# A limit of four on the weight transfers in flight in a streamed attention-and-mixer kernel

## Chip, cores and metric

One core of one Trainium2 chip. The metric is the device time of one execution in microseconds (us), as the median of several runs.

## The reference, cut to what matters

Four layers over 2048 tokens of width 640: attention with a recurrent memory, a token mixer with an MLP, and both again with the same weights. The attention works in 64 segments of 32 tokens, each one with 8 memory rows that come out of the segment before:

```python
for s in range(n_seg):                       # 64 segments, one after the other
    h = concat([mem, x[segment s]])          # 8 + 32 = 40 rows
    q, k, v = h @ Wq, h @ Wk, h @ Wv         # 32 heads of 192: 6144 columns each
    o = softmax(mask(q k^T * scale)) v @ Wo
    mem = o[:8]; outs.append(o[8:])
```

The four attention matrices together are 31 MB, and each segment needs all of them. The kernel keeps part of them resident on the core and streams the rest from HBM again in every step.

## The kernel before

The two attention layers run as two lanes, five segments apart, side by side in one step (80 columns); the first and last five steps have one lane (40 columns). All operations are first recorded with an engine, an estimated duration and a due time. A small list scheduler, the plan, then lays them out with a model of the transfers, and that order becomes each engine's program. Weights go through a ring of 8 slots. SyncE issues each transfer in the plan's order, as soon as the slot's former contents have been used.

```python
RING = 8
DMA_RATE = 345.0e3      # bytes per us in the plan
DMA_LAT = 2.2           # us
DMA_SKEW = 2.4          # us from the mean end of service to the last engine's landing
...
        def est(o, t):                       # earliest start of o in the plan
            s = max(t, o.ready)
            ...                              # and when its slots are free
...
            if o.dma:
                srv = max(s + DMA_LAT, srv) + o.dma / DMA_RATE
                done = srv + DMA_SKEW        # successors and slots count from here
...
            b = ring("ra")                   # streamed weights: 2 chunks of 128 x 768, 384 KB
            def fn(op):
                nc.sync.dma_start(out=T(b)[:, 0:2 * n].rearrange("p (c n) -> p c n", c=2), in_=w_src(kind, g, a, a + 2))
            add("SP", 0.45, due, fn, w=(b,), dma=P * 2 * n * 2, queue="wa")
...
    placed = plan.place()
    ctx.enter_context(tc.manual_schedule())
    for o in placed:
        o.fn(o)
```

## Time and profile before

| | before |
|---|---|
| median time | 3617.45 us (3604 to 3626) |
| span of the profiled run | 3600.4 us |
| middle stage, both lanes | 302 to 3299 us |
| transfers on SyncE's queue, all weights but two | 2941, one per 1.22 us |
| time from issue to landing | 5.3 us |

A transfer "lands" with the last of the sixteen increments of its semaphore, in the trace of before 1.95 us (median) after the first. "In flight" counts the transfers that are issued and not landed. "Idle" of TensorE is counted between one matmul's start and the next beyond the median distance for that form. I put it down to an instruction fetch where the instruction is the first of a block of 256 and no semaphore came in just before, and to weights where the last semaphore to come in was that of a weight transfer. The lines themselves stand in the prediction.

A line of waits reads: engine, what it writes, source line, then what ended the wait, then us in total, times, longest. PE is TensorE, PEld its weight loads, DVE VectorE, ACT ScalarE, POOL GpSimd, SPq SyncE issuing transfers. `wst` is a slot of the weight ring; `psq`, `psk`, `psv` and `psy` take the products with Wq, Wk, Wv and Wo, and `psh` and `y` those of the mixer. "issue" stands for idle time that nothing in the profile ended.

### The profile page before, as it was taken

What the parts mean: (1) busy time and instruction counts of PE and PEld (TensorE: products, weight loads), DVE (VectorE), ACT (ScalarE), POOL (GpSimd) and SP (SyncE); (2) the same over time, 40 slices, a digit from 0 to 9 for tenths busy, and PEclk for the clock granted to TensorE, in tenths of its full rate; (3) what the DMA queues carried; (4) which work ended last, traced back from release to release, by engine and by line L of the source; (5) the groups of instructions that cost most, each with busy time, mean ns of one, the idle gap of its engine ahead of it and who ended that gap; (6) DMA issues with size and microseconds to landing.
All of it is one profiled execution on the core that took longest, in us unless ns stands there. A gap on an engine that the chain in (4) does not pass through costs nothing.

```text
span 3600.4 us, 187964 instructions
## 1 busy us (share of the span) xinstructions
PE 3389.2 (94%) x84703; PEld 3261.4 (91%) x84703; DVE 2379.7 (66%) x7085; ACT 1703.7 (47%) x3584; POOL 305.4 (8%) x522
## 2 busy tenths in 40 slices
PE   5889999999999999999999999999999999999896
PEld 4778999999999999999999999999999999998785
DVE  2456766766666767666766677676767776676555
ACT  2344544544445555444545455554545554454432
POOL 2000000000000000000000000000000000000000
PEclk9999999999999999999999999999999999999998
DMA  9999999999999999999999999999999999999996
GB/s 343 301 307 311 304 304 299 310 301 303 297 307 314 311 298 309 300 301 305 315 308 309 298 304 313 308 307 307 308 311 311 313 309 301 301 307 310 297 314 211
DMA packets 804790, 1097.16 MB, mean 305 GB/s; under 512 B 51982, under 2 KB 800540, under 8 KB 803984
## 3 DMA queue, kind: packets, MB, share of 16 engines
q1 hardware_dynamic: 795472, 1069.06, 90.8%
q0 software_dynamic: 8512, 16.08, 1.4%
q8 instruction: 662, 10.85, 1.2%
q14 instruction: 144, 1.18, 0.1%
HBM read 1079.68 MB, written 8.19 MB: 302 GB/s over the span
## 4 chain that ended last, share of the span: by engine, by line
PE 89%; issue 5%; DMA 3%; DVE 1%; ACT 1%; SPq 0%; POOL 0%; POOLq 0%; ACTq 0%; DVEq 0%
PE psy L669 16%; PE psk L530 16%; PE psv L571 16%; PE psq L530 16%; PE psvt L583 5%; PE pso L650 5%; PE pss L602 4%; PE psh L993 3%; PE y L1011 3%; PE pst L635 2%; DMA wst<-in_A_Wq_dram 1%; PE psh L939 1%; PE hs L961 1%; DMA wst<-in_A_Wv_dram 1%; PE psv L755 1%
## 5 line engine op out<-in xcount | busy, mean ns | idle before, releaser
L656 DVE CAST oT<-pso 128x480 bf16<-128x480 f32 (+1 forms) x552 | 342.0, 620 | 478.0 <-PE pso L650 472.3
L587 ACT COPY V<-psvt 80x768 bf16<-80x768 bf16 (+1 forms) x552 | 438.4, 794 | 350.4 <-PE psvt L583 348.8
L530 PEld LDWEIGHTS <-wst 128*128 128x128 bf16 x13248 | 549.8, 100 | 37.4 <-issue 25.3
L669 PE MATMUL psy<-oT,wo 128*128 128x80 bf16 (+1 forms) x10350 | 499.6, 199 | 22.0 <-issue 14.8
L571 PE MATMUL psv<-hT,wv 128*128 128x80 bf16 (+1 forms) x9936 | 467.6, 199 | 15.7 <-issue 14.1
L530 PE MATMUL psq<-hT,wq 128*128 128x80 bf16 (+1 forms) x9936 | 463.4, 199 | 19.7 <-issue 12.7
L538 ACT CAST qT<-psq 128x480 bf16<-128x480 f32 (+1 forms) x552 | 292.1, 529 | 379.0 <-PE psq L530 375.6
L530 PE MATMUL psk<-hT,wk 128*128 128x80 bf16 (+1 forms) x9936 | 452.1, 199 | 19.0 <-issue 16.1
L577 ACT CAST vTs<-psv 128x480 bf16<-128x480 f32 (+1 forms) x552 | 291.8, 529 | 346.9 <-PE psv L571 340.9
L669 PEld LDWEIGHTS <-wo 128*128 128x128 bf16 x10350 | 418.7, 99 | 28.4 <-issue 20.6
L530 PEld LDWEIGHTS <-wk 128*128 128x128 bf16 x9936 | 398.2, 99 | 35.5 <-issue 21.4
L530 PEld LDWEIGHTS <-wq 128*128 128x128 bf16 x9936 | 400.6, 99 | 30.9 <-issue 14.4
L571 PEld LDWEIGHTS <-wv 128*128 128x128 bf16 x9936 | 400.3, 99 | 30.3 <-issue 16.6
L613 DVE CUSTOM_DVE_ANT_1 pss<-pss,mask 80x320 f32<-80x320 f32 (+1 forms) x512 | 245.0, 479 | 210.8 <-PE pss L602 206.4
L571 PE MATMUL psv<-hT,wst 128*128 128x80 bf16 (+1 forms) x6624 | 354.3, 199 | 13.0 <-issue 10.5
L530 PE MATMUL psk<-hT,wst 128*128 128x80 bf16 (+1 forms) x6624 | 349.8, 199 | 16.9 <-issue 12.9
L669 PE MATMUL psy<-oT,wst 128*128 128x80 bf16 (+1 forms) x6210 | 342.5, 199 | 6.9 <-issue 6.4
L530 PE MATMUL psq<-hT,wst 128*128 128x80 bf16 (+1 forms) x6624 | 331.8, 199 | 11.7 <-issue 7.4
L640 ACT COPY PT<-pst 80x320 bf16<-80x320 bf16 (+1 forms) x552 | 221.8, 402 | 249.3 <-PE pst L635 248.2
L625 DVE TENSOR_REDUCE sm<-pss 80x4 f32<-80x320 f32 (+1 forms) x552 | 252.1, 457 | 126.4 <-ACT pss L620 125.9
L546 DVE CAST kT<-psk 128x320 bf16<-128x320 f32 (+1 forms) x552 | 254.5, 461 | 105.4 <-PE psk L530 98.0
L620 ACT ACTIVATE pss<-pss,sm 80x320 f32<-80x320 f32 (+1 forms) x552 | 261.6, 474 | 123.1 <-DVE sm L613 123.0
(117 smaller groups left out, 5270.2 us busy)
## 6 DMA issues: line engine op xcount, KB each, us to landing
wst<-in_A_Wk_dram SPq DMA_DIRECT2D x552, 384.0 KB, 5.4
wst<-in_A_Wq_dram SPq DMA_DIRECT2D x552, 384.0 KB, 5.4
wst<-in_A_Wv_dram SPq DMA_DIRECT2D x552, 384.0 KB, 5.2
wst<-in_A_Wo_dram SPq DMA_DIRECT2D x621, 320.0 KB, 5.0
wst<-wbd SPq DMA_DIRECT2D x280, 320.0 KB, 5.2
wst<-in_B_w_dram SPq DMA_DIRECT2D x280, 320.0 KB, 5.8
wst<-wbd SPq DMA_DIRECT2D x70, 160.0 KB, 4.8
wk<-in_A_Wk_dram SPq DMA_DIRECT2D x8, 576.0 KB, 10.4
```

The lines of the kernel that those rows point to most:

```text
L530: nc.tensor.matmul(out=o[:, c, 0:N], lhsT=w[:, c * P:(c + 1) * P], rhs=h[:, kc, c0:c0 + N], start=pq.begin(), stop=True, skip_group_check= ...
L538: nc.scalar.copy(out=q[:, :, 0:N], in_=T(pq)[:, :, 0:N])
L546: nc.vector.tensor_copy(out=k4[:, :, 0::3, 0:N], in_=p4[:, :, 0::2, 0:N])
L571: nc.tensor.matmul(out=o[:, c, 0:N], lhsT=w[:, c * P:(c + 1) * P], rhs=h[:, kc, c0:c0 + N], start=pv.begin(), stop=True, skip_group_check= ...
L577: nc.scalar.copy(out=vs[:, :, 0:N], in_=T(pv)[:, :, 0:N])
L587: nc.scalar.copy(out=V_[0:N, :, 0:Dh], in_=T(pt)[0:N].rearrange("n c f -> n (c f)").rearrange("n (i e) -> n i e", i=HG))
L613: nc.vector.tensor_tensor_reduce(out=o, in0=o, in1=maskt.unsqueeze(1).to_broadcast([N, HG, N]), scale=-scale, scalar=3.0e38, op0=ALU.add, ...
L620: nc.scalar.activation(out=o, in_=o, func=ACT.Exp, bias=sm_[0:N, 0:1], scale=-1.0)
L625: nc.vector.reduce_sum(out=sm_[0:N, 4:4 + HG], in_=o, axis=AX.X)
L640: nc.scalar.copy(out=Pt[0:N, :, 0:N], in_=T(pst)[0:N, :, 0:N])
L656: nc.vector.tensor_copy(out=o_[:, :, 0:N], in_=T(pso)[:, :, 0:N])
L669: nc.tensor.matmul(out=T(psy[j])[:, m - m0, c0:c0 + N], lhsT=w[:, m * P:(m + 1) * P], rhs=o_[:, c, 0:N], start=psy[j].begin(), stop=True, ...
```

## The change

The intent, in the change's own words: "At most four weight transfers in flight: each waits for the landing of the fourth one ahead of it; placement plans with that". The plan also believes in an earlier landing (skew 1.0 instead of 2.4 us).

```diff
-DMA_SKEW = 2.4
+DMA_SKEW = 1.0
+FLIGHT = 4
...
         def est(o, t):
             s = max(t, o.ready)
+            if o.dma and o.e == "SP" and len(landed) >= FLIGHT:
+                s = max(s, landed[-FLIGHT])
...
                 done = srv + DMA_SKEW
+                if e == "SP":
+                    landed.append(done)
...  (each fn of a SyncE transfer now returns its instruction)
+    flight = []
     for o in placed:
-        o.fn(o)
+        ins = o.fn(o)
+        if o.dma and o.e == "SP":
+            if len(flight) >= FLIGHT:
+                tc.add_manual_dep(ins.ins, flight[-FLIGHT].ins.name,
+                                  mybir.DependencyInfo(mybir.DependencyClass.Sync, mybir.DependencyReason.DATA),
+                                  reason="transfers in flight")
+            flight.append(ins)
```

More of the change, by code (lines that the diff above doesn't have):

```diff
@@ L155, in place @@
         srv = 0.0
+        landed = []
         out = []
@@ L428, in fn @@
                 def fn(op):
-                    nc.sync.dma_start(out=tl[:], in_=w_src(kind, g, 0, cut))
+                    return nc.sync.dma_start(out=tl[:], in_=w_src(kind, g, 0, cut))
                 add("SP", 0.45, due, fn, w=(b,), dma=P * cut * n * 2, queue="wa")
@@ L438, in fn @@
             def fn(op):
-                nc.sync.dma_start(out=T(b)[:, 0:2 * n].rearrange("p (c n) -> p c n", c=2), in_=w_src(kind, g, a, a + 2))
+                return nc.sync.dma_start(out=T(b)[:, 0:2 * n].rearrange("p (c n) -> p c n", c=2), in_=w_src(kind, g, a, a + 2))
             add("SP", 0.45, due, fn, w=(b,), dma=P * 2 * n * 2, queue="wa")
@@ L462, in fn @@
             def fn(op):
-                nc.sync.dma_start(out=T(b)[:, 0:(e - a) * Dm].rearrange("p (c n) -> p c n", n=Dm), in_=src)
+                return nc.sync.dma_start(out=T(b)[:, 0:(e - a) * Dm].rearrange("p (c n) -> p c n", n=Dm), in_=src)
             add("SP", 0.45, due, fn, r=rd, w=(b,), dma=P * (e - a) * Dm * 2, queue="wb")
@@ L1052, in f1 @@
         def f1(op):
-            nc.sync.dma_start(out=xo[0:M, :], in_=A_mem0[0])
+            return nc.sync.dma_start(out=xo[0:M, :], in_=A_mem0[0])
         add("SP", 0.1, -90, f1, w=(B("xo"),), dma=20000)
@@ L1067, in f4 @@
         def f4(op):
-            nc.sync.dma_start(out=vb[:], in_=x0d[0:4 * SEG, :])
+            return nc.sync.dma_start(out=vb[:], in_=x0d[0:4 * SEG, :])
         add("SP", 0.1, -91, f4, w=(B("vb"),), dma=P * Dm * 2)
```

## The prediction

> **What bounds the kernel now.** I read the page first: the busy times, the 40 slices, the queues and the chain that ended last.
>
> ```profile
> PE 3389.2 (94%) x84703; PEld 3261.4 (91%) x84703; DVE 2379.7 (66%) x7085; ACT 1703.7 (47%) x3584; POOL 305.4 (8%) x522
> PE   5889999999999999999999999999999999999896
> DMA  9999999999999999999999999999999999999996
> GB/s 343 301 307 311 304 304 299 310 301 303 297 307 314 311 298 309 300 301 305 315 308 309 298 304 313 308 307 307 308 311 311 313 309 301 301 307 310 297 314 211
> q1 hardware_dynamic: 795472, 1069.06, 90.8%
> q8 instruction: 662, 10.85, 1.2%
> PE 89%; issue 5%; DMA 3%; DVE 1%; ACT 1%; SPq 0%; POOL 0%; POOLq 0%; ACTq 0%; DVEq 0%
> ```
>
> TensorE looks full, the DMA engines look full, and the chain is 89% TensorE, 5% "issue" and 3% DMA. The 5% is the surprise, so I looked for what TensorE waits for, in the long middle stage (302 to 3299 us from the start) where every step carries both lanes (80 columns):
>
> ```profile
> PEld L530 <- issue: 47.6, 61, 2.2
> PE psk L530 <- issue: 21.1, 32, 1.6
> PE psq L530 <- issue: 18.0, 22, 2.1
> PE psv L571 <- issue: 17.3, 27, 1.7
> PEld L530 <- DMA wst<-in_A_Wk_dram: 0.8, 2, 0.4
> ```
>
> Weights almost never arrive late (0.8 us in the largest such row); the idle time has no releaser at all. The timeline around 1011 us shows one of these gaps, in the middle of one run of matmuls from a resident weight tile:
>
> ```profile
> 1011.44 0.20 PE L571 MATMUL psv<-hT,wv 128*128 128x80 bf16 x1
> ...
> 1012.30 0.77 PE L571 MATMUL psv<-hT,wv 128*128 128x80 bf16 x17 [0.66 <-issue]
> 1012.31 0.63 PEld L571 LDWEIGHTS <-wv 128*128 128x128 bf16 x16 [0.76 <-issue]
> ```
>
> Nothing in the data can be late there, so I counted TensorE's instructions (weight loads and matmuls in order) and compared with the instruction queue, q8: 662 packets of 16 KB. TensorE has some 169,400 instructions; over 662 that is 256 each. Of the 150 gaps over 300 ns in the middle stage, 132, holding 112.8 of 119.4 us, sit exactly where one block of 256 ends and the next begins. They are instruction fetches that came late. Taking each form of matmul at its median start-to-start time, the middle stage holds 2861 us of matmuls in 2997 us; about 110 us of the missing 136 are fetch stalls, 2 us are waits for weights. In the two 40-column stages (104 to 302 and 3299 to 3498 us) fetch stalls are 20 and 19 us. So the whole kernel has about 150 us of them, 4% of its time.
>
> Next, the weight transfers themselves:
>
> ```profile
> SPq L439 <- PE psy L669: 346.7, 330, 3.6
> SPq L439 <- PE psv L571: 334.9, 331, 4.1
> SPq L439 <- DMA wst<-in_A_Wk_dram: 6.3, 14, 1.6
> ...
> wst<-in_A_Wk_dram SPq DMA_DIRECT2D x552, 384.0 KB, 5.4
> wst<-in_A_Wo_dram SPq DMA_DIRECT2D x621, 320.0 KB, 5.0
> ```
>
> SyncE, which issues them, waits for TensorE to give a ring slot back, hardly ever for another transfer. A transfer takes about 5.3 us to land. 2941 of them in 3600 us is one per 1.22 us, so on average 5.3 / 1.22 = 4.3 are in flight. Record by record (issue, and the last of the transfer's semaphore increments), an issue in the middle stage finds 4 or more ahead of it in 66% of cases (4: 37%, 5: 25%, 6: 3%). The landed weights then lie about 3.2 us (median) before TensorE's first wait on them.
>
> [...] 136 of 566 crossings of the middle stage stall by over 0.2 us, and a block of 256 runs in 5.1 us here. [...] the fetch of a block starts 1.3 to 3.3 us (10th to 90th percentile, median 2.3) after TensorE enters the block before it, never long before. [...] here a fetch starts later the more weights are in flight (below). [...]
>
> **The change, part by part.** (1) Each transfer on SyncE's queue waits for the landing of the fourth ahead. No data moves differently; the built program has the same number of instructions on each engine but for some 490 semaphore waits on SyncE, which is idle anyway (issues take 0.37 us of each 1.22). Two thirds of the issues are put off, by about the time until the oldest lands, some 0.5 us.
>
> What it removes is queue ahead of the fetch. For the 566 blocks of the middle stage, by weights in flight when TensorE enters the block before: with 3 in flight the fetch starts after 1.5 us and the mean stall is 52 ns (77 blocks); with 4, 2.0 us and 84 ns (196); with 5, 2.5 us and 293 ns (187); with 6, 2.7 us and 351 ns (87). A fetch takes 1.0 us and its block starts 1.2 us after it at the earliest, so in a block of 5.1 us a start later than 2.9 us stalls; the trace shows stalls from 2.6 us up. With at most 4, I take the mean of the 3 and 4 rows, 75 ns, against 193 now: 566 x 0.118 = 67 us. In the 40-column stages the same split is thinner; I take 15 of their 37 us. Together about 80 us off TensorE, which sets the end there.
>
> (2) The plan believes in an earlier landing: 1.4 us less (2.4 to 1.0). It therefore sets uses closer behind landings and counts on slots sooner. The order does change: 61% of TensorE's positions hold the same instruction. Of the 3.2 us of slack, 1.4 are planned away and about 0.5 are lost to the later issue, less what a shorter queue gives back. The early tail of slack (5% below 1.0 us, 10% below 1.4) turns into waits: I estimate 10% of 2941 transfers by 0.1 us, 30 us. (3) The real latency should fall to about 4.5 us, so the plan's new figure is nearer to the truth, and in the 40-column stages, where TensorE has 36 us of matmuls in a step of 49.5, a shorter slot cycle may give a few us: 10 us in all. Sum: 3617 - 80 + 30 - 10 = 3557; I round to 3550, as the author's smaller skew looks fitted.
>
> **The rivals.** *The limit itself becomes the bound.* With four in flight, one lands per latency / 4. Issues that now find 3 ahead just after a landing (137 of them) take 4.95 us: 1.24 us per transfer, against the 1.22 needed today and 1.19 for my time. All 2941 at 1.24 would be 3650 us plus the ends, about 3680. For it: DMA is at 9 tenths everywhere. Against it: with 4 or more ahead, landings follow each other at 1.12 us on average (median 1.08), so 4 x 1.12 = 4.5 us of queued work covers the lone latency of 3.3 us; and the windows show 369 to 372 GB/s between 20 and 80 us against 305 later, so the engines have reserve. *Nothing happens*: the fetch is held up by the DMA being full, not by the number in flight, and the rows with 5 and 6 merely mark busy moments. Then fetch stalls stay at 150 us and the time within 1% of 3617. The steady rise from row to row speaks for the queue, but it is a correlation. *The plan gains more*: if fetch stalls nearly vanish and 40-column steps shorten by 4 us each, 3617 - 140 - 40 = 3440.
>
> **Range and chances.** Fetch savings of 40 to 130 us and new weight waits of 0 to 80 span 3475 to 3650. The 2% line is at 3545, close to my point, so faster by over 2% and within 2% are near even, and the limit as the new bound keeps some chance of slower: 0.48, 0.40, 0.12.
>
> **What would show it.** Right: TensorE's "issue" idle time in the middle stage falls to about a third to a half; the median time to landing of 384 KB falls from 5.4 to 4.5 us; SyncE's waits name DMA landings in hundreds of rows; waits of TensorE for weights rise by tens of us, not hundreds. Wrong: "issue" stays while landings get quicker (then it was not the queue ahead), or TensorE's rows name "DMA wst" for over 100 us and GB/s falls below 300 (then the limit binds).

The figures are from the trace of before; in all 566 blocks of its middle stage the fetch began only after TensorE had entered the block ahead, by 0.24 us at the least. The lone latency of 3.3 us is a miscount: the trace shows 3.02 and 2.96 us.

## The result and the profile after

The changed kernel takes 3724.37 us (3715.65 to 3744.81, 4 runs) against 3618.78 us for the kernel before on the same chip: ratio 1.0305, 95% interval 1.0252 to 1.0358. Ratios here and below are the mean time of one kernel's fast runs over the mean of the other's in the same rounds, so not quite the ratio of the medians quoted. It is slower by 3%, outside my range of 3475 to 3650 us.

The page of the changed kernel, the same lines as those shown of before:

```profile
PE 3424.1 (92%) x84703; PEld 3279.1 (88%) x84703; DVE 2372.3 (64%) x7085; ACT 1717.9 (46%) x3584; POOL 306.0 (8%) x522
GB/s 323 305 300 302 299 295 294 297 296 301 307 301 290 295 290 292 292 293 297 294 296 297 294 299 296 304 295 296 297 301 292 289 297 297 296 305 300 304 298 202
PE 56%; DMA 40%; issue 2%; DVE 0%; POOL 0%; ACT 0%; SPq 0%; POOLq 0%; DVEq 0%
wst<-in_A_Wk_dram SPq DMA_DIRECT2D x552, 384.0 KB, 4.8
```

The chain that ended last now runs through DMA for 40% of the span, where it was 3%. Each transfer lands sooner (4.8 us, not 5.4), and yet the rate is lower in nearly every slice. "DMA" is a full row of nines in both pages, so that row would have shown nothing.

TensorE's waits in the changed kernel's middle stage (306 to 3401 us), then SyncE's waits over the whole run:

```profile
PE y L1017 <- DMA wst<-in_B_w_dram: 59.9, 35, 3.1
PE psh L999 <- DMA wst<-wbd: 30.3, 40, 2.0
PE psk L536 <- DMA wst<-in_A_Wk_dram: 26.8, 40, 1.7
PE psy L675 <- DMA wst<-in_A_Wo_dram: 23.0, 22, 2.6
...
PE psk L536 <- issue: 0.5, 1, 0.5
```

```profile
SPq L445 <- DMA wst<-in_A_Wq_dram: 342.5, 407, 3.3
SPq L445 <- DMA wst<-in_A_Wv_dram: 333.7, 406, 2.8
...
SPq L445 <- PE psy L675: 113.0, 167, 1.9
```

The "issue" rows of before are all but gone (0.5 us in the row for psk, where it was 21.1), and rows that name weights stand in their place (158 us together). SyncE, which waited for TensorE to give slots back, now waits for landings. (The line numbers are six higher in this kernel.)

Taken matmul by matmul, the middle stage shows both effects at full size:

| middle stage, us | before | after |
|---|---|---|
| length | 2997 | 3095 |
| matmuls at their median distance | 2861 | 2866 |
| late instruction fetches | 110.6 | 6.7 |
| late weights | 2.0 | 200.0 |
| ScalarE and VectorE | 16.1 | 2.7 |
| put down to none of these | 7 | 20 |

The matmuls at their median distance take 2860 to 2872 us in this stage in every run of this document, so TensorE's own pace explains none of the differences.

The middle stage thus loses 98 of the 114 us by which the profiled spans differ; the rest is in the ramp (4.8), the second 40-column stage (5.3) and the drain (5.5).

### The profile page after: what moved, and what is told of

It is laid out like the page before. It is cut to its first block, busy times and chain, and to the rows that moved or that the text cites. A ratio compares the mean times of both kernels' runs of the same rounds, so it can differ in the third digit from the quotient of the medians.

```text
span 3714.0 us, 188436 instructions
## 1 busy us (share of the span) xinstructions
PE 3424.1 (92%) x84703; PEld 3279.1 (88%) x84703; DVE 2372.3 (64%) x7085; ACT 1717.9 (46%) x3584; POOL 306.0 (8%) x522
## 3 DMA queue, kind: packets, MB, share of 16 engines
q14 instruction: 148, 1.21, 0.1%
## 4 chain that ended last, share of the span: by engine, by line
PE 56%; DMA 40%; issue 2%; DVE 0%; POOL 0%; ACT 0%; SPq 0%; POOLq 0%; DVEq 0%
PE psy L675 11%; DMA wst<-in_A_Wk_dram 11%; PE psv L577 10%; PE psq L536 9%; PE psk L536 9%; DMA wst<-in_A_Wq_dram 7%; DMA wst<-in_A_Wv_dram 7%; DMA wst<-in_B_w_dram 6%; DMA wst<-wbd 5%; DMA wst<-in_A_Wo_dram 5%; PE psvt L589 3%; PE pso L656 3%; PE pss L608 3%; PE y L1017 2%; PE psh L999 2%
## 5 line engine op out<-in xcount | busy, mean ns | idle before, releaser
L577 PE MATMUL psv<-hT,wv 128*128 128x80 bf16 (+1 forms) x9936 | 494.4, 199 | 4.6 <-issue 2.2
L675 PE MATMUL psy<-oT,wo 128*128 128x80 bf16 (+1 forms) x10350 | 491.6, 199 | 6.5 <-DMA wo<-in_A_Wo_dram 4.9
L536 PE MATMUL psk<-hT,wk 128*128 128x80 bf16 (+1 forms) x9936 | 473.3, 199 | 7.2 <-DMA wk<-in_A_Wk_dram 4.9
L577 PEld LDWEIGHTS <-wv 128*128 128x128 bf16 x9936 | 415.1, 99 | 19.5 <-DMA wv<-in_A_Wv_dram 3.3
L536 PEld LDWEIGHTS <-wk 128*128 128x128 bf16 x9936 | 407.3, 100 | 20.5 <-DMA wk<-in_A_Wk_dram 5.6
L577 PE MATMUL psv<-hT,wst 128*128 128x80 bf16 (+1 forms) x6624 | 343.4, 200 | 21.5 <-DMA wst<-in_A_Wv_dram 20.0
```

The lines of the kernel that those rows point to most:

```text
L536: nc.tensor.matmul(out=o[:, c, 0:N], lhsT=w[:, c * P:(c + 1) * P], rhs=h[:, kc, c0:c0 + N], start=pq.begin(), stop=True, skip_group_check= ...
L577: nc.tensor.matmul(out=o[:, c, 0:N], lhsT=w[:, c * P:(c + 1) * P], rhs=h[:, kc, c0:c0 + N], start=pv.begin(), stop=True, skip_group_check= ...
L675: nc.tensor.matmul(out=T(psy[j])[:, m - m0, c0:c0 + N], lhsT=w[:, m * P:(m + 1) * P], rhs=o_[:, c, 0:N], start=psy[j].begin(), stop=True, ...
```

## The experiments

Theory A: the wait itself caps the rate. With n in flight one transfer can land per (time to landing) / n, and with four this is more than TensorE needs. Theory B: the smaller skew makes the plan set uses too early, so that TensorE waits for weights whatever the limit. The first four runs take the two halves of the change apart and loosen the limit. In all of them the constant in the plan and that of the wait are separate:

```diff
-            if o.dma and o.e == "SP" and len(landed) >= FLIGHT:
-                s = max(s, landed[-FLIGHT])
+            if o.dma and o.e == "SP" and len(landed) >= PLAN_FLIGHT:
+                s = max(s, landed[-PLAN_FLIGHT])
```

"9999" below switches a limit off.

**Limit alone.** Every engine's instructions stand in the order of the kernel before (compared on all five engines); only the waits are added.

```diff
+PLAN_FLIGHT = 9999
+FLIGHT = 4
+DMA_SKEW = 2.4
```

> The old plan (skew 2.4, no limit in it), so every engine's order is that of the kernel before; only the wait for the landing of the fourth ahead is added. Theory A (the limit caps the rate: latency / 4): 3680 to 3740 us, median landing of 384 KB 4.8 us, TensorE's waits for weights in the middle stage 150 to 220 us, fetch stalls there under 15 us. Theory B (the new plan's smaller skew sets the uses too early): about 3550 us, fetch stalls gone as in the changed kernel, waits for weights under 30 us, because the old order keeps 3.2 us of slack.

Measured: 3692.61 us, ratio 1.0237 (1.0205 to 1.0270), as theory A had it in each number. In the middle stage TensorE waits 170.8 us for weights and 9.0 us for fetches. Landing takes 4.84 us on average, and 91% of the issues start within 0.15 us of the landing of the fourth ahead (median 0.063 us after it). The waits of TensorE in its middle stage:

```profile
PE psk L537 <- DMA wst<-in_A_Wk_dram: 57.4, 64, 2.2
PE psv L578 <- DMA wst<-in_A_Wv_dram: 34.6, 48, 1.5
PE y L1018 <- DMA wst<-in_B_w_dram: 25.5, 45, 1.5
...
PE psk L537 <- issue: 2.1, 4, 0.6
```

With an order that left the weights 3.2 us of slack, TensorE still waits. Theory A holds for most of the loss. The 3.2 us could not help: slack in the order is a head start, and a rate that is too low uses it up. Counted on the half of the transfers whose first wait the trace tells, the median time from landing to that wait is 3.2 us before and 1.4 us here.

**Plan alone.** The new plan with skew 1.0 and the limit in it, no wait on the chip.

```diff
+PLAN_FLIGHT = 4
+FLIGHT = 9999
 DMA_SKEW = 1.0
```

> The new plan and its order, without the wait. Theory A: no cap, so 3540 to 3630 us; landing about 5.3 us, fetch stalls in the middle stage 80 to 120 us as in the kernel before, waits for weights under 50 us. Theory B: 3700 us or more, with waits for weights of 200 us, since landings take longer than with the limit and the uses stand just as early.

Measured: 3624.77 us, ratio 1.0050 (1.0016 to 1.0085). Fetches 101.6 us, weights 40.2 us. TensorE's waits from 302 to 3299 us:

```profile
PE y L1018 <- DMA wst<-in_B_w_dram: 19.0, 30, 1.6
...
PE psk L537 <- issue: 17.7, 22, 1.9
```

So theory B has a small part: late weights come from the order alone, but far from 200 us of them. Limit alone (2.4%) and plan alone (0.5%) nearly add up to the whole (3.05%).

**Limit of five, then of six, in plan and wait.**

```diff
+PLAN_FLIGHT = 5      # 6 in the other
+FLIGHT = 5           # 6
 DMA_SKEW = 1.0
```

> Limit of five in both the plan and the wait, skew 1.0. Theory A: a latency near 5.3 us over five is 1.07 us per transfer, below the 1.2 that is needed, so the cap is off: waits for weights under 60 us, fetch stalls 20 to 80 us, time 3520 to 3600 us. Theory B: landings are later than with four and the uses as early: slower than the changed kernel, over 3720 us.

> Limit of six in both. Theory A: hardly any issue is held, so like plan alone: 3550 to 3630 us, fetch stalls 70 to 110 us, waits for weights under 40 us; not faster than five. Theory B: over 3720 us, as with five.

Measured with five: 3601.23 us, ratio 0.9985 (0.9955 to 1.0014), fetches 65.8 us, weights 58.4 us. With six: 3622.74 us, ratio 1.0043 (1.0013 to 1.0074), fetches 102.4 us, weights 43.5 us (I had said under 40). Theory B's forecast (over 3720 us) fails in both. One step in the limit takes the loss away, and the fetch stalls come back step by step. Five missed my 3520 to 3600 us by a hair. I put that down to the plan's late weights, some 40 us, which stayed; the next run tests it.

**Five with the old plan.** If those late weights are the plan's, the old plan with five should be free of both losses.

```diff
+PLAN_FLIGHT = 9999
+FLIGHT = 5
+DMA_SKEW = 2.4
```

> The kernel before plus a wait for the landing of the fifth ahead; plan and order unchanged. If the cap is latency / limit, it is (5.2 + 0.06) / 5 = 1.05 us per transfer and off; if the 40 us of weight waits in the plan-only run come from the smaller skew, they vanish here: waits for weights in the middle stage under 20 us, fetch stalls 50 to 75 us, time 3555 to 3595 us, ratio 0.985 to 0.995. If the waits come from the limit even at five, they stay near 58 us and the ratio is 1.0.

Measured over five rounds: 3560.14 us, ratio 0.9892 (0.9870 to 0.9914). Fetches 70.2 us, weights 4.7 us: faster than both kernels, as expected in each number. The gain over the kernel before is 1.1%, clear of the noise and still small: of the 110.6 us of fetch stalls more than half stay. Its "issue" rows in the middle stage, to be held against the prediction's rows of before (21.1, 18.0, 17.3):

```profile
PE psk L537 <- issue: 12.2, 20, 1.7
PE psv L578 <- issue: 11.4, 19, 1.4
PE psq L537 <- issue: 9.1, 13, 1.8
```

**Three with the old plan.** The strongest test of the cap as a rate.

```diff
+PLAN_FLIGHT = 9999
+FLIGHT = 3
+DMA_SKEW = 2.4
```

> The kernel before plus a wait for the landing of the third ahead. The cap theory gives a landing of 4.2 to 4.4 us and so (4.3 + 0.06) / 3 = 1.45 us per transfer, 4150 to 4350 us for 2941 of them, with fetch stalls under 5 us. If the loss with four were a matter of a few bad moments and not of the rate, three would cost a few per cent more only, under 3900 us.

Measured, one run: 4332.08 us (state unknown; its clock was 0.952 against 0.982 to 0.991 in the others' profiled runs, far too small a loss for a fifth of the time, and its matmuls at their median distance take 2872 us in the middle stage, as in the others). Fetches 0.5 us, weights 633.2 us. From the DMA view of this run:

```profile
GB/s 289 257 252 255 252 253 251 255 254 257 251 250 254 251 248 250 254 258 258 262 253 254 252 255 249 256 258 259 258 256 252 255 253 253 254 259 254 252 251 191
wst<-in_A_Wk_dram SPq DMA_DIRECT2D x552, 384.0 KB, 4.3
```

The rate is flat at some 253 GB/s from end to end: a cap, not bad moments. The old-plan runs stand in one table, counted in the middle stage. "Cap" is (mean time to landing + 0.06 us from a landing to the next issue) / n; "held" is the share of issues that start within 0.15 us of the landing they wait for.

| n in flight | landing, us | cap, us | measured us per transfer | held |
|---|---|---|---|---|
| 3 | 4.29 | 1.45 | 1.458 | 97% |
| 4 | 4.84 | 1.22 | 1.238 | 91% |
| 5 | 5.17 | 1.05 | 1.196 | 39% |
| no limit, before | 5.29 | - | 1.210 | - |

At three and four the measured distance is the cap to within 1.5%. At five the cap is off and TensorE sets the pace. From 500 to 3000 us four moved 299 GB/s and five 309. (In the changed kernel 85% of the issues are held, the cap is 1.21 us and the distance 1.248 us: there the plan's late weights come on top.)

**Four and five in turn.** A try at four and a half.

```diff
-            if len(flight) >= FLIGHT:
+            ahead = FLIGHT + len(flight) % 2
+            if len(flight) >= ahead:
```

> Old plan; the limit is four for every second transfer and five for the others. If fetch stalls follow the queue ahead and weight waits follow the cap, both lie between those of four and of five with the old plan: cap about 1.13 us, weight waits 20 to 80 us, fetch stalls 20 to 50 us, 3550 to 3620 us. No theory of mine makes it much better than five.

Measured: 3721.08 us, ratio 1.0330 (1.0307 to 1.0352), weights 191.4 us, fetches 21.2 us. My expectation was wrong, and the edit is why: a transfer that waits for the fifth ahead of it waits for the very landing that the one before it (fourth ahead) has already waited for, and SyncE issues in order. None of those issues was held; 93% of the others were. The transfers went out in pairs at the pace of four, (4.90 + 0.06) / 4 = 1.24 us, measured 1.252. It says nothing about four and a half.

**Five, the plan knows, old skew.**

```diff
+PLAN_FLIGHT = 5
+FLIGHT = 5
+DMA_SKEW = 2.4
```

> Limit of five in plan and wait, skew 2.4 as before. As five with the old plan if the plan's own limit matters little: 3550 to 3600 us, weight waits under 30 us. If the limit in the plan is what makes it ask too early, waits near 58 us as with skew 1.0 and a ratio of 1.0.

Measured: 3575.72 us, ratio 0.9926 (0.9906 to 0.9947), fetches 76.2 us, weights 1.5 us. With skew 1.0 and the same limits it was 58.4 us of weights, so those came from the skew, not from the limit in the plan.

**Six with the old plan.**

```diff
+PLAN_FLIGHT = 9999
+FLIGHT = 6
+DMA_SKEW = 2.4
```

> The kernel before plus a wait for the landing of the sixth ahead; old plan. Few issues are held: fetch stalls in the middle stage 80 to 110 us, waits for weights under 10 us, ratio 0.993 to 1.0, that is between no limit and five. If it is as good as five, then it is not the queue ahead of the fetch that five shortens.

Measured: 3601.45 us, ratio 0.9990 (0.9961 to 1.0019), fetches 94.4 us, weights 3.1 us. The gain of five is gone. This run carries 461 added wait instructions on SyncE, against 490 with four, so the instructions themselves cost nothing that shows.

**Four, the plan knows, old skew.** Can a careful plan hide the cap?

```diff
+PLAN_FLIGHT = 4
+FLIGHT = 4
+DMA_SKEW = 2.4
```

> Limit of four in plan and wait, but with the old skew of 2.4. Theory A (the cap is in the wait itself): no plan can help, 3670 to 3710 us, weight waits in the middle stage 150 to 200 us. If a plan that knows of the limit and is careful about landings can hide it, under 3620 us.

Measured: 3759.12 us, ratio 1.0423 (1.0402 to 1.0444). This is slower than I had expected, and in another way: TensorE hardly waits for weights at all in the middle stage, but 263 us for ScalarE and VectorE. So one more run.

**The same plan without the wait.**

```diff
+PLAN_FLIGHT = 4
+FLIGHT = 9999
+DMA_SKEW = 2.4
```

> The plan of the run before (limit of four in the plan, skew 2.4), without the wait on the chip. If that plan's order is what makes TensorE wait for ScalarE and VectorE, these waits (263 us in the middle stage with the wait) stay, at 150 to 270 us, and the time is 3650 to 3760 us although nothing is held. If they were the cap seen in another place, the time returns to 3600 to 3650 us with waits for ScalarE and VectorE under 50 us.

Measured: 3771.55 us, ratio 1.0469 (1.0422 to 1.0517), 12 us above my range, with 260 us of waits for ScalarE and VectorE. TensorE's waits in its middle stage:

```profile
PE pso L657 <- ACT V L594: 40.1, 90, 0.8
PE psy L676 <- DVE oT L663: 26.3, 73, 0.4
PE pst L642 <- DVE Pm L634: 20.3, 56, 0.4
```

The order alone does it. My reading of why, from the plan's code and not from a run: with a landing of 2.2 + 1.14 + 2.4 = 5.7 us in the plan's own constants and four in flight, the plan reckons with one transfer per 1.43 us and lays out TensorE for a machine that slow; on the chip TensorE then comes to the attention's steps (V, oT, Pm above) before their inputs are there. This also bears on why the change lowers the skew: with 1.0 the plan reckons with 4.34 / 4 = 1.09 us. That figure avoids such an order and is wrong the other way, since the chip needs 4.80 us to land and 1.22 per transfer.

## Why the prediction was wrong

**What bounds the kernel, and what the wait removes: right in kind, too small in size.** The 5% "issue" were late instruction fetches, and a shorter queue of weights removes them. In the limit-alone run, where nothing but the waits differs, a fetch starts 1.40 us (median) after TensorE enters the block before, against 2.26, and the middle stage's stalls fall from 110.6 to 9.0 us. In the changed kernel they fall by 104 us, where I had said 67. I had taken 75 ns per block from the rows with 3 and 4 in flight; the changed kernel shows 17 ns. The rows of before were too pessimistic: with 4 in flight at the trigger, the fetch started after 2.03 us there and after 1.50 us in the changed kernel. I had guessed that 4 were then often the rest of 5 or 6. The trace of before does not bear it out: 104 of these 196 blocks had had no more than 4 in flight in the 1.5 us before, and their fetch started after 2.10 us, the others' after 2.0. So it stays open. The rival that the number in flight does not matter falls: three, four, five, six and no limit give 0.5, 9.0, 70.2, 94.4 and 110.6 us of fetch stalls with the old plan, and five and no limit run at nearly the same rate (309 and 307 GB/s from 500 to 3000 us).

**The step that failed is the dismissal of the first rival**, "so 4 x 1.12 = 4.5 us of queued work covers the lone latency of 3.3 us". I took the distance of landings while a long queue was there and assumed that four in flight would keep that queue. They do not: landing takes 4.80 us in the changed kernel, 4.84 with the limit alone. My other figure, 4.95 us for the issues that found three ahead just after a landing, was nearly it. The trace of before held a better one, which I did not take: sorted by the number ahead at the issue, its transfers in the middle stage land after 4.32 us (two ahead, 175 of them), 4.77 (three, 658) and 5.37 (four, 934) on average. Under limits of three, four and five it came to 4.29, 4.84 and 5.17. And the page of before already held the need: 1.22 us per transfer with 150 us of TensorE stalls in it. A cap of 1.22 to 1.24 cannot carry a kernel that is to become faster. From 1.24 I had worked out 3680 us for this rival, 44 us under what came.

**The term of the sum that was mis-sized** is therefore the new waits for weights, "I estimate 10% of 2941 transfers by 0.1 us, 30 us". They came to 200 us in the middle stage alone. I treated them as the tail of a distribution of slack, which is right for a delay that happens once to each transfer. A rate that is short by 2% lets each delay stand and adds the next, until TensorE runs at the rate of the transfers (with the limit alone one per 1.238 us, against a cap of 1.22). Of those 200 us the runs put 171 with the limit alone and 40 with the plan alone.

**The early-landing part** was right in direction: the order from the smaller skew does cause waits, 40 us without any wait on SyncE. The 10 us of gain in the 40-column stages did not come: together they are 401 us against 397.

**The signs I had named** told the cases apart. Landings at 4.8 us where I said 4.5, SyncE naming landings in hundreds of waits, "DMA wst" rows on TensorE that add up to 158 us (the largest is 59.9) and GB/s under 300 (296 from 500 to 3000 us): the last two were my stated signs that the limit binds.

**Three readings of the prediction do not hold**, and none of them moved its result. In "15 of their 37 us" the parts are 20 and 19, so 39. Of weights, only two transfers found nothing ahead of them, both in the drain, and they landed after 3.02 and 2.96 us. The 3.3 us of the prediction is what a count gives that leaves out the 368 transfers for which `prof` finds no landing: nine then seem to be alone, with a median of 3.31 us. And the 490 waits on SyncE are not the only new instructions: the changed kernel's trace also has 89 more waits on VectorE, 46 fewer on ScalarE and 61 fewer on TensorE, which come with the new order: the limit-alone run, with the old one, shows none of them.

**What stays open**: what a landing of 4.8 us at four in flight is made of. With the limit alone, a transfer between whose first and last increment an instruction fetch runs lands after 4.99 us on average and the others after 4.68; but a transfer that takes longer over its increments also has more chance to meet a fetch. Counted over the same stretch for each (2 to 4 us after its issue) it is 4.90 against 4.77. That the fetches are a part of it is not shown. And no run shows a limit between four and five.

## What to carry to other kernels

A limit on transfers in flight was a limit on the rate here: take the time to landing at that depth (the profile without the limit gave it to within 4%, sorted by the number ahead at the issue), add the reaction of the issuing engine, divide by the number, and compare with the time per transfer that the kernel needs after the hoped-for gain, not before it. Slack between landing and use (3.2 us here) did not help against a rate that was too low. The long queue of weights also delayed TensorE's instruction fetches (they started 2.26 us by median after TensorE entered the block before, against 1.40 with a limit of four), which showed as idle time that no semaphore ended; with the old plan a limit of five gained 1.1% and a limit of four lost 2.4%. When the wait and the planner's model change together, test them apart: the plan's belief moved the time by up to 4.7% with no wait at all.
